# Thirteen blocks of 512 rows with seven products each, behind the 60th pair of a routed feed-forward kernel

## The chip, the cores and the metric

The kernel runs on one core of one Trainium2 chip. The metric is the device time of one execution in microseconds, lower is better. All arithmetic is in fp32.

## The reference, cut to what matters

The input `x` has 8 sequences of 3,584 tokens with 192 channels. A causal convolution of 7 taps, with softmax weights per head of 24 channels, gives each token a row. A gate then picks one of 8 experts for each token, and the row goes through that expert's two matrices.

```python
logits = np.einsum('bsd,de->bse', x, w_gate)                  # x: rows after the convolution
local_gate = 1/(1 + np.exp(-np.einsum('bsd,de->bse', x, w_local).squeeze(-1)))
# per sequence, in order of s:
e = fresh_e if s == 0 or local_gate[b, s] < 0.5 else prev_e   # fresh_e = argmax of logits
h = np.maximum(x[b, s] @ w1[e], 0.0)                          # 192 -> 1024
out[b, s] = p[e] * (h @ w2[e])                                # 1024 -> 192, p = softmax(logits)
```

There are 28,672 tokens. How many go to each expert depends on the data (3,081 to 4,253 with the inputs given).

## The kernel before

**Two kinds of work share the core.** The main work is the experts' two matrix products, on TensorE. The side work is the convolution, the routing and the sorting of rows by expert; it runs mostly on VectorE, with ScalarE, GpSimd and some small TensorE products.

**Side work.** The tokens come in 16 parts of 1,792. The first two have a start of their own. From the third on, `conv(g)` (line 387, VectorE, with a first tap on ScalarE) makes the rows of part g, and `route(g)` computes logits: four transposes `z` on VectorE (line 570), small products on TensorE (line 580), copies `ls` on ScalarE (line 585) and a transpose `lq` on VectorE (line 588). A long run of small VectorE instructions then finds each row's place. `put` scatters rows to the DRAM buffer `slots` by indirect DMAs of GpSimd (line 775), sorted by expert in units of 128 rows. `table` writes, at fixed points, which units are full by then, so that blocks can be formed before all tokens are known.

**Main work.** A block is one unit (a single) or two units (a pair) of one expert. Every block loads the whole of its expert's weights `wb` (1.5 MB) and its rows `xg`; loads are asked for three blocks ahead by SP, at indices read from the tables. The list of blocks is fixed in the program: 35 singles, 87 pairs, 20 singles, and 2 spare singles that are skipped when nothing is left for them.

For each block:

- `turn` transposes the rows on TensorE (line 359) and ScalarE copies them into `xT` (line 949), one block ahead.
- `hidden` (line 963) multiplies by the first matrix. The 192 channels are three chunks of 64; the two halves of the array, 64 rows each, compute two halves of the 1,024 hidden columns side by side. ScalarE's relu (line 968) writes `hT`.
- `output` (line 980) multiplies by the second matrix. ScalarE scales one half's sum into `o_sb` (line 988), VectorE adds the other half (line 992), and GpSimd sends each unit to its tokens' places in `out` (line 996).

PSUM has two banks for `xps`, four for `hps` and two for `yps`.

**Order.** Each engine's order is written out by hand. `step(time)` issues side work up to a budget in nominal microseconds; it is called behind `hidden`, inside `output` (1.2) and behind `output`:

```python
        step(2.4 if i == 0 else 2.1 if n == 1 else 4.2)
        output(n, wbs.pop(i), xgs.pop(i), hT)
        if i == 0:
            rest(route1)
        step(1.3 if n == 1 else 3.0)
```

`put` is issued behind a relu or a copy of the block, one to three times per pair. `ensure` asks for a block's rows, and issues more side work if a part that they need isn't placed.

Of the kernel before, what the change touches and what calls it, by code (L numbers as in the profile page):

```python
# [17 lines left out]
P = 128  # L18
# [4 lines left out]
N = B * S  # L23
# [13 lines left out]
FK = F // P  # L37
BT = 2 * UT
KT = BT // P
CAPU = N // UT  # L40
CAP = CAPU * UT
NU = (N + E * (UT - 1)) // UT
# [8 lines left out]

ONE = [_sure(min(g + 1, EARLY) * PT, UT) for g in range(NPART)]
TWO = [_sure((g + 1) * PT - ONE[-1] * UT, BT) if g >= EARLY else 0 for g in range(NPART)]


HALF = 0.5
FULL = {0: ONE[0], HALF: _sure(PT + PT // 2, UT), **{g: ONE[g] for g in range(1, NPART)}}
REST = NU - ONE[-1] - 2 * TWO[-1]  # L60
DG = 3 + D
Y0 = 2
IX = DG - 1
# [18 lines left out]
def kernel(  # L82
# [20 lines left out]
    hp = ctx.enter_context(tc.tile_pool(name="hp", bufs=1))  # L103
    op = ctx.enter_context(tc.tile_pool(name="op", bufs=2))
    xps_p = ctx.enter_context(tc.tile_pool(name="xps_p", bufs=1, space=PSUM))
    hps_p = ctx.enter_context(tc.tile_pool(name="hps_p", bufs=4, space=PSUM))
    yps_p = ctx.enter_context(tc.tile_pool(name="yps_p", bufs=2, space=PSUM))
    ctx.enter_context(tc.manual_schedule())


# [168 lines left out]
                            base=0, pattern=[[1, P]], channel_multiplier=-1)  # L279
    ii = cst.tile([P, E], I32, name="ii")  # L280
    nc.gpsimd.iota(ii, pattern=[[1, E]], base=0, channel_multiplier=0)
    pi = cst.tile([P, 2], I32, name="pi")
    nc.gpsimd.iota(pi, pattern=[[0, 2]], base=0, channel_multiplier=1)
    ti0 = cst.tile([P, NT], I32, name="ti0")
    nc.gpsimd.iota(ti0, pattern=[[1, NT]], base=0, channel_multiplier=NT)
    ef = cst.tile([P, E], F32, name="ef")
# [6 lines left out]
    nc.gpsimd.tensor_scalar(eb, ef, float(CAPU), None, Alu.mult)  # L293
    ec = cst.tile([P, E], F32, name="ec")
    nc.gpsimd.tensor_scalar(ec, ef, float(CAP), -1.0, Alu.mult, Alu.add)
    pf = cst.tile([P, 2], F32, name="pf")
    nc.gpsimd.tensor_copy(pf, pi)
    nc.gpsimd.tensor_tensor(pf[:, 1:], pf[:, 1:], pf[:, :1], op=Alu.add)
    i_of = pf[:, 0:1]
    tb0 = cst.tile([P, NB], I32, name="tb0")  # L300
    nc.gpsimd.iota(tb0, pattern=[[TB, NB]], base=0, channel_multiplier=1)
# [32 lines left out]
    pad = cst.tile([P, DG], F32, name="pad")  # L334
    nc.gpsimd.memset(pad, 0.0)
    nc.gpsimd.memset(pad.bitcast(I32)[:, IX:], N)
    nc.sync.dma_start(out=slots[DUMMY * UT:(DUMMY + 1) * UT], in_=pad)


    base = cst.tile([P, E], F32, name="base")  # L340
# [2 lines left out]
    nc.gpsimd.memset(used, 0.0)  # L343


    tab = [cst.tile([P, 3], F32, name=f"tab{k}") for k in range(3)]
    ends = [cst.tile([P, 1 + E], F32, name=f"ends{k}") for k in range(3)]
    for k in range(3):
        nc.gpsimd.memset(tab[k], 0.0)
        nc.gpsimd.memset(ends[k], 0.0)  # L350
    tabi = {}
# [402 lines left out]
    def tables(g):  # L754
        if ONE[g] > (ONE[g - 1] if g else 0):
            yield from table(0, g, 1, ONE[g])
        if TWO[g] > (TWO[g - 1] if g else 0):
            yield from table(1, g, 2, TWO[g])
        if g == NPART - 1:
            yield from table(2, g, 1, None)  # L760
            yield from fill(g)

    to_put = []
# [21 lines left out]
        tc.add_to_no_dep_group("puts", ins)  # L785
        tc.add_to_no_dep_group(f"puts{g}", ins)

    def table(kind, g, size, cap):


        end = ends[kind]
        new = sm.tile([P, E], F32, name="new")
        ni = sm.tile([P, E], I32, name="ni")
        nc.vector.scalar_tensor_tensor(new, used, -float(UT), base, Alu.mult, Alu.add)
        yield 0.2
        if cap is None:
            nc.vector.tensor_scalar(new, new, float(UT - 1), None, Alu.add)
            yield 0.2
        nc.vector.tensor_copy(ni, new)
        yield 0.2  # L800
        nc.vector.tensor_scalar(ni, ni, (UT * size).bit_length() - 1, None, Alu.arith_shift_right)
        yield 0.2
        nc.vector.tensor_copy(new, ni)
        yield 0.2
        nc.vector.tensor_copy(end[:, 0:1], end[:, E:])
        yield 0.2
        nc.vector.tensor_tensor_scan(end[:, 1:], new, new, end[:, 0:1], Alu.add, Alu.max)
        yield 0.2
        if cap is not None:
            nc.vector.tensor_scalar(end, end, float(cap), None, Alu.min)  # L810
            yield 0.2
        inn = sm.tile([P, E], F32, name="inn")
        nc.vector.tensor_scalar(inn, end[:, :E], i_of, None, Alu.is_le)
        yield 0.2
        nc.vector.scalar_tensor_tensor(inn, end[:, 1:], i_of, inn, Alu.is_gt, Alu.mult)
        yield 0.2

        row = sm.tile([P, E], F32, name="row")
        nc.vector.scalar_tensor_tensor(row, end[:, :E], -float(size), used, Alu.mult, Alu.add)
        yield 0.2  # L820
        nc.vector.tensor_tensor(row, row, eb, op=Alu.add)
        yield 0.2
        add = sm.tile([P, 3, E], F32, name="add")
        nc.vector.scalar_tensor_tensor(add[:, 0, :], row, pf[:, size - 1:size], inn,
                                       Alu.add, Alu.mult)
        yield 0.2
        nc.vector.tensor_tensor(add[:, 1, :], ef, inn, op=Alu.mult)
        yield 0.2
        nc.vector.tensor_copy(add[:, 2, :], inn)
        yield 0.2  # L830
        sums = sm.tile([P, 3], F32, name="sums")
        nc.vector.tensor_reduce(sums, add, axis=AX.X, op=Alu.add)
        yield 0.2
        nc.vector.tensor_tensor(tab[kind], tab[kind], sums, op=Alu.add)
        yield 0.2
        ti = cst.tile([P, 2], I32, name=f"tabi{kind}_{int(2 * g)}")
        if cap is None:

            no = sm.tile([P, 1], F32, name="no")
            nc.vector.tensor_scalar(no, tab[kind][:, 2:3], -float(DUMMY), float(DUMMY),  # L840
                                    Alu.mult, Alu.add)
            yield 0.2
            nc.vector.tensor_tensor(tab[kind][:, 0:1], tab[kind][:, 0:1], no, op=Alu.add)
            yield 0.2
        nc.vector.tensor_copy(ti, tab[kind][:, 0:2])
        yield 0.2
        tabi[kind, g] = ti
        nc.vector.tensor_tensor(new, end[:, 1:], end[:, :E], op=Alu.subtract)
        yield 0.2
        nc.vector.scalar_tensor_tensor(used, new, float(size), used, Alu.mult, Alu.add)  # L850
        yield 0.2

    def fill(g):
# [25 lines left out]
        nc.vector.tensor_copy(toi, to)  # L879
        yield 0.2  # L880
        for e in range(E):
            to_put.append((g, pad, toi[:, e:e + 1]))


    blocks = [(0, 1, i, next(g for g in FULL if i < FULL[g])) for i in range(ONE[-1])]
    blocks += [(1, 2, i, next(g for g in range(NPART) if i < TWO[g])) for i in range(TWO[-1])]
    blocks += [(2, 1, i, NPART - 1) for i in range(REST)]

    AHEAD = 3

# [15 lines left out]

    def load_rows(i):
        n, group = blocks[i][1], blocks[i][3]
        r = entry(i, 0, DUMMY + 1 - n)
        xg = xp.tile([P, KT, DG], F32, name="xg")  # L910
        get = nc.sync.dma_start(
            out=xg[:, :n, :].rearrange("p k d -> p (k d)"),
            in_=slots.rearrange("(r p) d -> r (p d)", p=UT)[bass.ds(r, n)]
            .rearrange("o (p x) -> (o p) x", x=n * DG))
        if group not in waited:
            waited.add(group)
            for g, ins in puts:
                if g == group:
                    tc.add_manual_dep(get.ins, ins.name, SYNC, reason="a row of the block")
        for g in FULL:  # L920
            if g > group and any(p[0] == g for p in puts):
                tc.declare_no_dep(get.ins, group=f"puts{g}", reason="not in a unit full before")
        tc.add_to_no_dep_group("gets", get.ins)
        return xg
# [48 lines left out]
    def output(n, wb, xg, hT):  # L973
# [11 lines left out]
        o_sb = op.tile([P, KT, D], F32, name="o_sb")  # L985
        y = [[yps[half][:, k * D:(k + 1) * D] for half in range(2)] for k in range(n)]
        for k in range(n):
            nc.scalar.activation(o_sb[:, k, :], y[k][0], Act.Copy, scale=xg[:, k, 0:1])  # L988

        step(1.2 if n > 1 or st["block"] else 0)  # L990
        for k in range(n):
# [9 lines left out]
            tc.add_to_no_dep_group("sent", sent.ins)  # L1001


    LEAD = 2
    LATE = 3
    st = {"block": 0, "conv": 1, "cgen": None, "route": 1, "rgen": None, "routed": 1}
# [23 lines left out]
    def route_op():  # L1030
        c = next(st["rgen"], None)
        if c is None:
            st["rgen"] = None
            st["routed"] = st["route"]
        return c

    def step(time):
# [26 lines left out]
    def rest(work):  # L1064
        for _ in work:
            pass
# [38 lines left out]
            wbs[j] = load_w(j)  # L1105
            loaded[0] += 1

    spare = blocks[len(blocks) - SPARE:]
    del blocks[len(blocks) - SPARE:]
    loaded = [0]  # L1110
    weights(AHEAD - 1)

# [25 lines left out]
    for i, (_, n, _, _) in enumerate(blocks):  # L1138
        st["block"] = i
        ensure(i)  # L1140
        weights(i + AHEAD)
        if i == LATE:
            x_in[3] = load_x(3)
        hT = hidden(n, wbs[i], xT, (1, 1) if i else (0, 0))
        if i + 1 < len(blocks):
            xT, copied = turn(blocks[i + 1][1], xgs[i + 1])
            if len(to_put) > NT // 2 and n == KT:
                put(copied)
        step(2.4 if i == 0 else 2.1 if n == 1 else 4.2)
        output(n, wbs.pop(i), xgs.pop(i), hT)  # L1150
        if i == 0:
            rest(route1)
        step(1.3 if n == 1 else 3.0)

    kind, _, at, group = spare[0]
    any_left = nc.values_load(tabi[kind, group][at:at + 1, 0:1], min_val=0, max_val=DUMMY,  # L1156
                              skip_runtime_bounds_check_because="an entry of the table")
    with tc.If(any_left < DUMMY):
        for block in spare:
            blocks.append(block)  # L1160
            i = len(blocks) - 1
            n = block[1]
            xg = load_rows(i)
            wb = load_w(i)
            xT, _ = turn(n, xg)
            output(n, wb, xg, hidden(n, wb, xT))


def _w1_layout(np, w1):
# [64 lines left out]
```

## Time and profile before

| | before |
|---|---|
| median of 3 runs | 1314.7 us (1314.69 to 1315.19) |
| profiled execution | 1326.81 us, its span 1325.1 us |
| granted TensorE clock, mean | 0.998 |
| TensorE matmul busy | 1304.4 us, 98% of the span |
| VectorE busy | 778.3 us, 59% |
| ScalarE busy | 625.2 us, 47% |
| GpSimd busy | 480.4 us, 36% |
| first pair begins, last single begins | 260.1 us, 1312.7 us |
| last side work on VectorE ends | 965.2 us |
| DMA | 325 MB, mean 245 GB/s |

A share of busy time is a mean over stages. Matmuls are pipelined and overlap, so the busy time of TensorE is no measure of how much it computes; the distance from one block's first weight load to the next's is. A group's row gives the line, the engine, the tile written and those read, the shape, the count, then the total and mean (ns) of its time, and the idle time of the engine just ahead of it with what ended it.

### The profile page before, as it was taken

The numbers are of one execution on the slowest core, as the hardware profiler recorded it, in microseconds if no ns is written. First come the engines' busy times: TensorE is split into PE (matmuls) and PEld (weight loads), VectorE is DVE, ScalarE is ACT, GpSimd is POOL, SyncE is SP. The second block draws the span as 40 slices with busy tenths as digits, with TensorE's granted clock in tenths as the row PEclk, the third lists the DMA queues.
The fourth block names the chain that finished last, engine by engine and source line by source line (L and its number), as shares of the span: only waits on it lengthen the run. The fifth ranks groups of instructions, "written<-read, shape, count | busy, mean of one in ns | idle before, by whom it ended". The sixth has DMA issues, their size and how long they took to land. (4 is left out here: it accounts for less than half of the span.)

```text
span 1325.1 us, 41356 instructions
## 1 busy us (share of the span) xinstructions
PE 1304.4 (98%) x16682; PEld 1260.9 (95%) x16682; DVE 778.3 (59%) x2434; ACT 625.2 (47%) x1571; POOL 480.4 (36%) x520
## 2 busy tenths in 40 slices
PE   9899999999999999999999999999999999999997
PEld 7799999999999999999999999999999999999997
DVE  6888898977878787878777878785610000000000
ACT  5345555544454545444545454544444444444553
POOL 4445352534343434343434343434344212211111
PEclk9999999999999999999999999999999999999999
DMA  5789999967575757575757575756565555556893
GB/s 188 283 349 391 376 365 345 394 213 266 182 275 177 290 188 277 201 260 192 271 186 273 193 271 199 267 195 210 197 211 205 189 185 188 192 187 229 313 317 131
DMA packets 67298, 325.29 MB, mean 245 GB/s; under 512 B 12576, under 2 KB 38103, under 8 KB 47650
## 3 DMA queue, kind: packets, MB, share of 16 engines
q1 hardware_dynamic: 44784, 277.41, 58.4%
q0 software_dynamic: 22320, 45.22, 9.2%
q8 instruction: 133, 2.18, 0.7%
q14 instruction: 59, 0.48, 0.1%
q10 hardware_dynamic: 2, 0.00, 0.0%
HBM read 277.29 MB, written 45.77 MB: 244 GB/s over the span
## 5 line engine op out<-in xcount | busy, mean ns | idle before, releaser
L980 PE MATMUL yps<-wb,hT 64*128 64x192 f32 x7328 | 641.0, 325 | 5.8 <-ACT hT L968 2.8
L963 PE MATMUL hps<-xT,wb 64*128 64x256 f32 (+1 forms) x6816 | 637.2, 336 | 1.7 <-issue 1.4
L963 PEld LDWEIGHTS hps<-xT,wb 64*128 64x128 f32 x6816 | 589.1, 187 | 27.2 <-issue 4.0
L980 PEld LDWEIGHTS yps<-wb,hT 64*128 64x128 f32 x7328 | 602.8, 187 | 11.1 <-issue 4.6
L996 POOL DMA_INDIRECT out_dram<-o_sb,xg x229 | 232.3, 1014 | 605.7 <-DVE o_sb L992 533.9
L968 ACT ACTIVATE hT<-hps 128x512 f32<-128x512 f32 (+1 forms) x568 | 261.9, 512 | 361.4 <-PE hps L963 246.5
L387 DVE SCALAR_TENSOR_TENSOR y_sb<-x_sb,c,y_sb 128x336 f32<-128x336 f32 x672 | 376.5, 570 | 18.9 <-issue 0.8
L992 DVE SCALAR_TENSOR_TENSOR o_sb<-yps,xg,o_sb 128x192 f32<-128x192 f32 x229 | 87.5, 414 | 467.8 <-ACT o_sb L988 461.4
L775 POOL DMA_INDIRECT slots<-y_sb,posi x228 | 231.2, 1014 | 209.3 <-ACT xT L949 114.8
L988 ACT ACTIVATE o_sb<-yps,xg 128x192 f32<-128x192 f32 x229 | 86.9, 418 | 289.8 <-PE yps L980 287.4
L949 ACT COPY xT<-xps 64x256 f32<-64x256 f32 (+4 forms) x568 | 210.8, 371 | 11.7 <-issue 1.7
L377 ACT ACTIVATE y_sb<-x_sb,c 128x336 f32<-128x336 f32 x112 | 63.7, 581 | 0.0
L359 PEld LDWEIGHTS xps<-ident,xg 64*128 64x128 f32 (+1 forms) x916 | 57.0, 124 | 5.2
L359 PE MATMUL xps<-ident,xg 64*128 64x64 f32 (+1 forms) x916 | 60.0, 217 | 0.0
L570 DVE STREAM_TRANSPOSE z<-y_sb 128x768 f32<-128x768 f32 (+1 forms) x56 | 45.4, 853 | 0.4
L596 DVE COPY lt<-lq 32x36 f32<-32x36 f32 x224 | 40.8, 182 | 3.5
L580 PE MATMUL hps<-z,wg 64*32 64x128 f32 x1344 | 24.2, 272 | 1.2 <-issue 1.2
L580 PEld LDWEIGHTS hps<-z,wg 64*32 64x32 f32 x1344 | 19.2, 105 | 4.1 <-issue 2.9
L556 PE MATMUL yps<-y_sb,hot 112*128 112x194 f32 x64 | 12.6, 353 | 1.4 <-DVE hot L550 1.1
L556 PEld LDWEIGHTS yps<-y_sb,hot 112*128 112x128 f32 x64 | 11.3, 202 | 2.1 <-DVE hot L550 1.6
L672 DVE COPY bk<-so_far 1x32 f32<-1x32 f32 x56 | 12.3, 220 | 0.7
L588 DVE STREAM_TRANSPOSE lq<-ls 128x256 f32<-128x256 f32 x14 | 6.2, 441 | 10.9 <-ACT ls L585 10.9
(236 smaller groups left out, 358.0 us busy)
## 6 DMA issues: line engine op xcount, KB each, us to landing
wb<-in_w_dram SPq DMA_DIRECT2D x138, 1536.0 KB
x_sb<-in_x_dram SPq DMA_DIRECT2D x14, 1920.0 KB
xg<-slots SPq DMA_DIRECT2D x87, 195.0 KB
wb<-in_w_dram SPq DMA_DIRECT2D x12, 512.0 KB
xg<-slots SPq DMA_DIRECT2D x53, 97.5 KB
out_dram<-o_sb,xg POOLq DMA_INDIRECT x229
slots<-y_sb,posi POOLq DMA_INDIRECT x228
x_sb<-in_xb_dram SPq DMA_DIRECT2D x4, 768.0 KB
```

The source lines that it names most:

```text
L359: nc.tensor.transpose(to, src[rows], identity=ident[rows, rows])
L377: nc.scalar.activation(cols(h), chans(h, 0), Act.Copy, scale=c[:, h, 0:1])
L387: nc.vector.scalar_tensor_tensor(cols(h), chans(h, k), c[:, h, k:k + 1], cols(h), Alu.mult, Alu.add)
L570: nc.vector.transpose(z[:, t:u, :], y_sb[:, t:u, Y0:Y0 + D])
L775: ins = nc.gpsimd.indirect_dma_start(out=slots[:, :], in_=rows, in_offset=None, out_offset=bass.IndirectOffsetOnAxis(ap=to, axis=0)).ins
L949: copied = nc.scalar.copy(a, b)
L963: nc.tensor.matmul(hps[half][:, j, w], lhsT=wb[rows, f0:f0 + P], rhs=xT[rows, d, w], start=(d == 0 and j == 0), stop=(d == KD - 1), skip_g ...
L968: relu = nc.scalar.activation(hT[:, m:m + 2, w], hps[half][:, :, w], Act.Relu)
L980: nc.tensor.matmul(yps[half][:, k * D:(k + 1) * D], lhsT=hT[rows, m, k * P:(k + 1) * P], rhs=wb[rows, WA + m * D:WA + (m + 1) * D], start= ...
L988: nc.scalar.activation(o_sb[:, k, :], y[k][0], Act.Copy, scale=xg[:, k, 0:1])
L992: nc.vector.scalar_tensor_tensor(o_sb[:, k, :], y[k][1], xg[:, k, 0:1], o_sb[:, k, :], Alu.mult, Alu.add)
L996: sent = nc.gpsimd.indirect_dma_start(out=out, in_=o_sb[:, k, :], in_offset=None, out_offset=bass.IndirectOffsetOnAxis(ap=xg.bitcast(I32)[ ...
```

## The change

The list of blocks becomes 35 singles, 60 pairs, 13 quads (4 units, 512 rows, one expert), 4 pairs, 14 singles. 20 spare singles follow behind two nested conditions, for data on which fewer quads or pairs fill up. Three tables are made at the end of routing instead of one.

In a quad the first two of the three channel chunks, two halves of its rows and two halves of the hidden columns of each array half form a product of 2 x 2 sub-matrices. It is computed by Strassen's method in Winograd's form: seven products of sums instead of eight. The third chunk stays four plain products. `combine_w` (GpSimd) forms the sums of weights, partly in place in `wb`; `combine_x` (VectorE) forms those of rows; ScalarE copies partial results out of PSUM, and VectorE adds them. From the first quad on the pools of `hps` and `yps` are closed and three tiles of two banks each, `late_p`, take their place; `xps` also takes one of the products. `xT`, the sums and the hidden pieces live in the two buffers of `x_sb` and in a buffer of `y_sb`, and rows in a ring of four places in another. The singles and pairs behind the quads use `hidden_late` and `output_late` on these buffers.

So that routing ends before the first quad, pairs issue side work with budgets of 4.8, 1.2 and 3.6 instead of 4.2, 1.2 and 3.0, and up to one more `put`.

```diff
+PAIRED = 60
+TWO = [min(PAIRED, _sure((g + 1) * PT - ONE[-1] * UT, BT)) if g >= EARLY else 0
+       for g in range(NPART)]
...
-        if g == NPART - 1:
-            yield from table(2, g, 1, None)
+        if g == LAST:
+            yield from table(2, g, 4, FOUR, 0)
+            yield from table(3, g, 2, PAIRS, 0)
+            yield from table(4, g, 1, None)
             yield from fill(g)
...
-blocks += [(2, 1, i, NPART - 1) for i in range(REST)]
+blocks += [(2, 4, i, LAST) for i in range(FOUR)]
+blocks += [(3, 2, i, LAST) for i in range(PAIRS)]
+blocks += [(4, 1, i, PADS) for i in range(REST)]
...
+    def combine_w(wb):
+        wt = room["wt"].rearrange("p (k s) -> p k s", k=3)
+        b11, b12, b21, b22 = [wb[:, k * 2 * P:(k + 1) * 2 * P] for k in range(4)]
+        nc.gpsimd.tensor_tensor(wt[:, 1, :], b22, b12, op=Alu.subtract)
+        yield
+        nc.gpsimd.tensor_tensor(b12, b12, b11, op=Alu.subtract)
+        yield
+        nc.gpsimd.tensor_tensor(wt[:, 0, :], b22, b12, op=Alu.subtract)
+        yield
+        nc.gpsimd.tensor_tensor(wt[:, 2, :], b21, wt[:, 0, :], op=Alu.subtract)
+        yield wt
...
+        nc.vector.tensor_tensor(xc[:, 0, :], xT[:, 0, one], xT[:, 0, two], op=Alu.subtract)
+        nc.vector.tensor_tensor(xT[:, 0, two], xT[:, 0, two], xT[:, 1, two], op=Alu.add)
+        nc.vector.tensor_tensor(xc[:, 1, :], xT[:, 0, two], xT[:, 0, one], op=Alu.subtract)
+        nc.vector.tensor_tensor(xc[:, 2, :], xT[:, 1, one], xc[:, 1, :], op=Alu.subtract)
+        nc.vector.tensor_tensor(xc[:, 3, :], xT[:, 2, one], xT[:, 2, two], op=Alu.subtract)
...
+        def times(to, a, b, first=False):
+            for j in range(2):
+                for half, rows in halves():
+                    ins = nc.tensor.matmul(to[:, half, j, :], lhsT=b[rows, j * P:(j + 1) * P],
+                                           rhs=a[rows, :], start=(first and j == 0), stop=True,
+                                           skip_group_check=True)
+            return ins
+
+        times(xb, a11, b11, True)
+        nc.scalar.copy(h11, xb)
+        times(yb, s1, t1, True)
+        times(yb, a23, b32)
+        nc.scalar.copy(h22, yb)
+        times(xb, s2, t2)
+        nc.scalar.copy(h12, xb)
+        put(times(wbk, a12, b21, True))
+        times(wbk, a13, b31)
+        nc.vector.tensor_tensor(h11, wbk, h11, op=Alu.add)
+        nc.scalar.activation(h11, h11, Act.Relu)
+        put(times(xb, s3, t3))
+        nc.vector.tensor_tensor(h22, xb, h22, op=Alu.add)
+        nc.scalar.activation(h22, h22, Act.Relu)
+        times(yb, s4, b22)
+        put(times(yb, s5, b32))
+        at = turn_next()
+        times(xb, a22, t4)
+        wt = weights_next()
+        next(wt)
+        put(times(xb, a23, b31))
+        next(wt)
+        nc.vector.tensor_tensor(h12, yb, h12, op=Alu.add)
+        nc.scalar.activation(h12, h12, Act.Relu)
+        nc.scalar.activation(h21, xb, Act.Relu)
+        return [[h11, h12], [h21, h22]], at, wt
...
-            step(2.4 if i == 0 else 2.1 if n == 1 else 4.2)
+            step(2.4 if i == 0 else 2.1 if n == 1 else 4.8)
...
-        step(1.3 if n == 1 else 3.0)
+            step(1.3 if n == 1 else 3.6)
+            continue
+        if i == FIRST:
+            banks.close()
+            for k in range(3):
+                late_p.append(ctx.enter_context(tc.tile_pool(name=f"late{k}", bufs=1, space=PSUM)))
```

`output_late` computes the output of a quad in two parts of two units each, with one tile of two banks per part; between the parts it calls `combine_x` for the next quad and issues the last step of `combine_w`.

## The prediction

> **What bounds the kernel now.** I read the busy shares and slices of the page first, then the table of waits, then the order of instructions inside one block, and last the groups of a stretch in which side work runs.
>
> ```profile
> PE 1304.4 (98%) x16682; PEld 1260.9 (95%) x16682; DVE 778.3 (59%) x2434; ACT 625.2 (47%) x1571; POOL 480.4 (36%) x520
> ...
> PE   9899999999999999999999999999999999999997
> ...
> DVE  6888898977878787878777878785610000000000
> ```
>
> TensorE is full in every slice; VectorE carries routing and convolution until slice 29 and then idles. Between 260 and 965 us the table of waits has for TensorE's matmuls only 0.9 us. A share alone would not settle it, since busy matmuls overlap, so here is the order of weight loads in one late pair (start, length, engine, line) and in one late single:
>
> ```profile
> 1048.88 5.10 PEld L963 LDWEIGHTS hps<-xT,wb 64*128 64x128 f32 x48
> 1054.01 0.45 PEld L359 LDWEIGHTS xps<-ident,xg 64*128 64x128 f32 x8
> 1054.40 5.18 PEld L980 LDWEIGHTS yps<-wb,hT 64*128 64x128 f32 x64
> 1059.55 0.57 PEld L963 LDWEIGHTS hps<-xT,wb 64*128 64x128 f32 x6
> ```
>
> ```profile
> 1296.39 2.81 PEld L963 LDWEIGHTS hps<-xT,wb 64*128 64x128 f32 x48
> 1299.12 0.23 PEld L359 LDWEIGHTS xps<-ident,xg 64*128 64x128 f32 x4
> 1299.29 2.58 PEld L980 LDWEIGHTS yps<-wb,hT 64*128 64x128 f32 x32
> 1301.84 0.35 PEld L963 LDWEIGHTS hps<-xT,wb 64*128 64x128 f32 x3
> ```
>
> A pair takes 1059.55 - 1048.88 = 10.67 us without a hole: 5.13 hidden, 0.39 turning, 5.15 output. The hidden part is 48 matmuls; the two 64-row halves run side by side, so 24 slots of 5.13/24 = 0.214 us for 256 columns. A single takes 5.445 us, against 5.333 for half a pair. So in the part that is changed time is what TensorE must stream, and nothing else.
>
> [...] In the trace the three accumulating steps of a hidden half all run at one pace. [...]
>
> **The change, part by part.**
>
> *Removed and added TensorE work.* Behind pair 60 there are 74 units of 128 rows: before 27 pairs and 20 singles, after 13 quads, 4 pairs and 14 singles (routing the reference's inputs fills all 13 quads and 4 pairs, so the spare blocks stay skipped). Two pairs need 12 hidden products of 256 rows by 256 hidden columns by 64 channels; `seven` issues 11. A product is 2 x 2 matmuls, two passes each, so 4 slots: 4 x 0.214 = 0.855 us. A quad is 11 x 0.855 = 9.40, turning 2 x 0.39 = 0.78, output 2 x 5.15 = 10.30: 20.48 us against 21.33. 13 x 0.855 = **11.1 us** gained, all on TensorE's path. Six singles fewer: 6 x (5.445 - 5.333) = **0.7 us**. The 14 logit insertions (1.8 us each) stay.
>
> *Can the evictions keep pace inside a quad?* The accumulator `xb` is read after the 1st and 4th product and overwritten by later ones. What ScalarE does in the pair above:
>
> ```profile
> 1049.24 0.73 ACT L988 ACTIVATE o_sb<-yps,xg 128x192 f32<-128x192 f32 x2 [2.59 <-PE yps L980]
> 1051.89 1.08 ACT L968 ACTIVATE hT<-hps 128x512 f32<-128x512 f32 x2 [1.92 <-PE hps L963]
> 1054.42 1.08 ACT L968 ACTIVATE hT<-hps 128x512 f32<-128x512 f32 x2 [1.45 <-PE hps L963]
> 1055.39 1.75 ACT L949 COPY xT<-xps 128x256 f32<-128x256 f32 x4
> ```
>
> It starts 0.36 to 0.45 us after TensorE is through; 512 elements take 0.54 us, 256 in the late singles 0.33, so 1,024 some 0.96 (estimate). From a quad's start: product 1 ends at 0.86, copy 1.26 to 2.22; product 4 is due at 2.57. Product 3 ends at 2.57, copy 2.97 to 3.93; product 4 ends at 3.42, copy 3.93 to 4.89; product 7 is due at 5.13. Margins: 0.3 and some 0.15 us with 0.1 us from ScalarE back to TensorE. [...] ScalarE's sum: 7 x 0.96 + 2.6 turning + 1.5 output = 10.8 of 20.5 us.
>
> *GpSimd's `combine_w`.* No such row exists. [...] the nearest row, the one-input copy of 512 (line 223), takes 0.655. Four per quad beside four indirect DMAs of 1.0 us: 7 of 20.5 us, each a block ahead of its reader except the fourth, written behind the first two sends and read 9 us later. Even at 2 us each it stays covered. I take nothing; bounds 0 and 0.3 us a quad.
>
> So a quad loses 0 to 0.3 us at product 7; I take 0.08, **1.1 us** in all (bounds 0 and 4).
>
> *Moved: the side work.* Per pair 4.8 + 1.2 + 3.6 = 9.6 units are issued instead of 8.4, so the last routing stands six pairs ahead of the first quad (before: 23 pairs ahead of the singles), a part per five pairs instead of six. VectorE over six pairs and one part, 469 to 534.66 us:
>
> ```profile
> L387 DVE SCALAR_TENSOR_TENSOR y_sb<-x_sb,c,y_sb 128x336 f32<-128x336 f32 x48 | 26.9, 569 | 1.3
> ...
> L992 DVE SCALAR_TENSOR_TENSOR o_sb<-yps,xg,o_sb 128x192 f32<-128x192 f32 x12 | 4.5, 413 | 11.5 <-ACT o_sb L988 11.5
> ```
>
> It is occupied 65.66 - 11.5 = 54.2 us. With ten evictions instead of twelve (0.37 each) 53.4 us remain, 55 if the gaps under 0.12 us between instructions count in full; TensorE needs 5 x 10.67 + 1.83 = 55.2. VectorE goes from 83% to 97-99% and still does not bind; the eviction may lag 3.7 us (output of the next block starts 5.5 us later, the eviction ends 1.6 us after its block) before TensorE waits. The 14 scatters per five pairs cost GpSimd 24 x 1.3 = 31 of 55 us. I take 0 (bounds -1 and +15).
>
> *Boundary, DMA, start.* Reused row buffers and PSUM banks were freed several pairs earlier; the first quad's rows (390 KB) are asked for some 15 us before they are turned. SP's weight loads queue behind row loads that now wait for the sends of the block before last: about 3 us of delay in a lead of three blocks (16 us among singles), so no cost. Weights moved fall from 47 x 1.5 to 31 x 1.5 MB. At the start GpSimd gets four memsets (0.1 us each) and a little arithmetic, beside waits of 4.7 us there; the pad rows grow by 290 KB. Together 0 (bounds -0.5 and +1.5).
>
> **Sum.** 11.1 + 0.7 - 1.1 = 10.7 us. The profiled execution took 1326.8 us (span 1325.1, 1.7 around it), the median without profile 1314.7, 0.9% less; scaled, 10.6. **Predicted 1304 us**; the profiled span should be near 1314.5.
>
> **Rivals.**
> 1. *VectorE becomes the bound of the pair stage, slower.* Place: evictions at line 992 of pairs 1 to 49. For it: 97-99% in the sum, and the logits' transpose now stands directly behind an eviction, where it waits about 1.2 us for TensorE and ScalarE. Against: lag may reach 3.7 us, and convolution rows cost 0.57 us whether GpSimd is busy or not. It decides once a part needs over 55.2 us; all gain is gone at 56.4 (ten parts x 1.2). At 5% more than 55 (57.8) ten parts lose 26, less the lag, some 22: 1326 us.
> 2. *The quads stall at the evictions.* If a copy takes 1.3 us instead of 0.96, product 7 waits 0.6 us, 13 x 0.6 = 8: about 1311. For it: the smallest margin; against: the slope from 256 to 512 elements.
> 3. *Whole-tile dependences.* `xT`, `xc` and `wt` share one row buffer. If a reader of one waited for writers of the others, `combine_w` (last part behind the sends) would hold up each quad by a few us: 1320 or more. The built program's waits name the right engines only at products 2, 4 and 10, which speaks against it.
>
> **Numbers.** Forecast 0.70; a gain over it (pair-stage hiccups of some 2 us go away) 0.02; rival 2, partly or in full, 0.15 (0.03 of it within 0.2%); rival 1 0.10 (0.03 still faster, 0.02 within, 0.05 slower); rival 3 0.03, slower. 0.2% (2.6 us) is about what a measurement of this kernel can tell from no change. Slower by more: 0.08; within: 0.05; faster: 0.87. The range reaches from all margins holding with some gain to rival 2 in full: 1300.5 to 1311.
>
> **What would show it.** Weight loads of the changed kernel's line 1152 (88 per quad) in 9.4 us without waits; quads 20.5 us apart; the first gap at product 7, released by ScalarE's copy of `h12`, if any. Pairs still 10.67 us, and idle before VectorE's eviction (now line 1030) nearly gone in that stage. It is wrong if pairs are longer than 10.7 us (rival 1), if product 10 waits for VectorE, or if quads exceed 21.3 us.

## The result, and the profile after

| | before | after |
|---|---|---|
| median without profile | 1314.7 us (1313.93 to 1315.19, 4 runs) | 1304.16 us (1303.46 to 1305.35, 4 runs) |
| ratio, 95% interval | | 0.9921 (0.9904 to 0.9938) |
| profiled execution, its span | 1326.8, 1325.1 us | 1305.35, 1303.6 us |

The time fell by 10.5 us; 10.7 were forecast. That agreement has to be read with care. Run again on chips 10, 7 and 1, the same two kernels gave ratios of 1.0004, 0.9964 and 1.0007 (below; the chip of this first comparison is not on record), so the gain of the quads is certain and what the denser side work costs is not. The two profiled executions lie 21.5 us apart, the medians 10.5, and the span, forecast near 1314.5 us, is 1303.6. That forecast scaled from the profile before, which took 12 us more than the median before, while the profile after took 1 us more than the median after; so the two profiles can hardly have been taken in like conditions. Of the 21.5 us, 7.6 stand ahead of the first pair (252.5 us after, 260.1 before), where other traces of one and the same kernel differ as much. So I compare by stages.

The busy row and two rows of slices of the page after:

```profile
PE 1284.2 (99%) x16434; PEld 1220.6 (94%) x16434; DVE 846.3 (65%) x2526; ACT 651.1 (50%) x1482; POOL 523.1 (40%) x577
...
PE   9899999999999999999999999999999999999997
...
DVE  5989898988988899998999996801333333330000
```

TensorE stays full; its matmuls overlap (in the quads 376 ns each, eight of them in 0.85 us). VectorE's side work ends in slice 26 instead of 29, at a higher level; the row of 3 behind it is the work in the quads.

One quad in the timeline after (start, length, engine, line; PEld is a weight load, 187 ns each):

```profile
1012.17 2.51 PEld L1152 LDWEIGHTS ps<-x_sb,wb 64*128 64x128 f32 x24
1013.46 1.01 ACT L1158 COPY x_sb<-ps 128x1024 f32<-128x1024 f32 x1 [0.18 <-PE ps L1152]
1014.71 0.84 PEld L1152 LDWEIGHTS ps<-x_sb 64*128 64x128 f32 x8
1015.19 1.01 ACT L1161 COPY y_sb<-ps 128x1024 f32<-128x1024 f32 x1 [0.71 <-PE ps L1152]
1015.57 1.70 PEld L1152 LDWEIGHTS xps<-x_sb,wb 64*128 64x128 f32 x16
1016.10 1.02 ACT L1163 COPY x_sb<-ps 128x1024 f32<-128x1024 f32 x1
1017.30 0.84 PEld L1152 LDWEIGHTS ps<-x_sb 64*128 64x128 f32 x8
...
1018.64 0.73 POOL L1115 TENSOR_TENSOR x_sb<-wb 128x256 f32<-128x256 f32 x1 [2.36 <-PE ps L1152]
...
1018.93 1.21 DVE L1169 TENSOR_TENSOR y_sb<-ps,y_sb 128x1024 f32<-128x1024 f32 x1
...
1019.89 0.68 PEld L383 LDWEIGHTS xps<-ident,y_sb 64*128 64x128 f32 x16
...
1022.13 7.88 PEld L1196 LDWEIGHTS ps<-wb,x_sb 64*128 64x128 f32 x96
```

A bracket gives the idle time ahead of a row and what ended it. No PEld row has one: TensorE never waits in the quad. The copy at line 1163 ends at 1017.12 and product 7, which adds onto the accumulator that this copy reads, begins at 1017.30: the predicted narrow place, with a margin of 0.18 us. VectorE's second add (line 1169), which reads the same accumulator behind product 7, ends at 1020.14, and product 10, which adds onto it again, begins at 1020.51: 0.37 us. Adding onto what stands in a bank costs nothing extra here: products 1 to 3, of which the third adds onto the second, take 2.54 us (0.85 each), product 4, which adds onto the first, 0.86. From 1012.17 to 1022.13 are 9.96 us for hidden part and turning, the output takes 10.46; the next quad's first load comes 20.42 us after this one's, and so it is between all 13.

VectorE's groups over five pairs and one part, 428.46 to 483.5 us after (count, then busy us and mean ns, then the idle time ahead of them):

```profile
L411 DVE SCALAR_TENSOR_TENSOR y_sb<-x_sb,c,y_sb 128x336 f32<-128x336 f32 x48 | 26.8, 570 | 2.4 <-ACT y_sb L401 1.1
L1030 DVE SCALAR_TENSOR_TENSOR o_sb<-yps,xg,o_sb 128x192 f32<-128x192 f32 x11 | 4.1, 407 | 0.2 <-ACT o_sb L1024 0.2
```

The eviction's 11.5 us of waiting are down to 0.2: in this stretch VectorE is always behind, as forecast. It waits for 1.3 us in all, so that it is occupied for 53.7 us, and the part still takes 55.04 us, which is TensorE's time. In the first 50 pairs VectorE's eviction starts 0.46 us behind ScalarE's in the trace before, and 0.97 us in the trace after (medians; at most 2.2).

### The profile page after: what moved, and what is told of

It reads as the page before. It is cut to its first block, busy times and chain, and to the rows that moved or that the text cites. A ratio compares the mean times of both kernels' runs of the same rounds, so it can differ in the third digit from the quotient of the medians.

```text
span 1303.6 us, 40830 instructions
## 1 busy us (share of the span) xinstructions
PE 1284.2 (99%) x16434; PEld 1220.6 (94%) x16434; DVE 846.3 (65%) x2526; ACT 651.1 (50%) x1482; POOL 523.1 (40%) x577
## 3 DMA queue, kind: packets, MB, share of 16 engines
q8 instruction: 131, 2.15, 0.7%
## 4 chain that ended last, share of the span: by engine, by line
PE 96%; DVE 3%; issue 0%; POOL 0%; POOLq 0%; ACT 0%; DVEq 0%
PE yps L1016 31%; PE hps L999 31%; PE ps L1196 15%; PE ps L1152 8%; PE ps L1103 4%; PE xps L383 2%; PE xps L1152 2%; PE hps L604 2%; DVE y_sb L411 1%; PE hps L233 1%; PE hps L178 0%; DVE hot L574 0%; PE hps L256 0%; PE yps L264 0%; DVE run L475 0%
## 5 line engine op out<-in xcount | busy, mean ns | idle before, releaser
L1016 PE MATMUL yps<-wb,hT 64*128 64x192 f32 x4960 | 429.8, 325 | 3.2 <-DVE o_sb L1030 2.4
L999 PE MATMUL hps<-xT,wb 64*128 64x256 f32 (+1 forms) x4560 | 425.9, 338 | 1.9 <-DVE at L503 1.2
L999 PEld LDWEIGHTS hps<-xT,wb 64*128 64x128 f32 x4560 | 378.7, 188 | 33.9 <-issue 3.9
L1016 PEld LDWEIGHTS yps<-wb,hT 64*128 64x128 f32 x4960 | 405.7, 187 | 4.6 <-DVE o_sb L1030 2.7
L411 DVE SCALAR_TENSOR_TENSOR y_sb<-x_sb,c,y_sb 128x336 f32<-128x336 f32 x672 | 375.6, 569 | 28.4 <-ACT y_sb L401 10.5
L1004 ACT ACTIVATE hT<-hps 128x512 f32<-128x512 f32 (+1 forms) x380 | 176.4, 516 | 244.5 <-PE hps L999 244.5
L1214 POOL DMA_INDIRECT out_dram<-o_sb,y_sb x74 | 76.4, 1032 | 237.5 <-DVE o_sb L1209 218.7
L1196 PE MATMUL ps<-wb,x_sb 64*128 64x192 f32 x1952 | 165.0, 323 | 0.0
L1196 PEld LDWEIGHTS ps<-wb,x_sb 64*128 64x128 f32 x1952 | 159.3, 187 | 0.6
L985 ACT COPY xT<-xps 128x256 f32<-128x256 f32 (+3 forms) x380 | 142.0, 374 | 10.6 <-PE xps L383 4.8
L1152 PEld LDWEIGHTS ps<-x_sb,wb 64*128 64x128 f32 x624 | 59.0, 187 | 7.3
L1103 PEld LDWEIGHTS ps<-x_sb,wb 64*128 64x128 f32 x864 | 59.4, 188 | 0.9 <-issue 0.2
```

What stands on the lines that cost most here:

```text
L411: nc.vector.scalar_tensor_tensor(cols(h), chans(h, k), c[:, h, k:k + 1], cols(h), Alu.mult, Alu.add)
L985: copied = nc.scalar.copy(a, b)
L999: nc.tensor.matmul(hps[half][:, j, w], lhsT=wb[rows, f0:f0 + P], rhs=xT[rows, d, w], start=(d == 0 and j == 0), stop=(d == KD - 1), skip_g ...
L1004: relu = nc.scalar.activation(hT[:, m:m + 2, w], hps[half][:, :, w], Act.Relu)
L1016: nc.tensor.matmul(yps[half][:, k * D:(k + 1) * D], lhsT=hT[rows, m, k * P:(k + 1) * P], rhs=wb[rows, WA + m * D:WA + (m + 1) * D], start= ...
L1103: nc.tensor.matmul(hps[:, half, j, :], lhsT=wb[rows, f0:f0 + P], rhs=xT[rows, d, :], start=(d == 0 and j == 0), stop=(d == KD - 1), skip_g ...
```

## The stages of all traces

Read from the first weight loads of the blocks. "Extra" is what the pairs ahead of the first quad (or, before, ahead of the 61st pair) take over 10.67 us each and 1.78 us for each logits insertion; "rest" runs from there to the last matmul, "tail" from the last matmul to the end of the span. A dash stands where no chip is on record.

| trace | chip | early singles | pairs | extra | rest | tail |
|---|---|---|---|---|---|---|
| before | - | 213.9 | 659.1 | 2.9 | 399.1 | 6.8 |
| after | - | 207.9 | 657.6 | -0.4 | 384.4 | 9.1 |
| b1_before | 7 | 217.3 | 659.3 | 3.1 | 399.8 | 6.8 |
| a2_after | 7 | 218.2 | 665.5 | 7.5 | 385.6 | 9.1 |
| a1_after | 10 | 218.7 | 669.5 | 11.5 | 385.3 | 8.9 |
| a3_after | 1 | 220.3 | 669.8 | 11.8 | 385.1 | 8.9 |
| e2_pace | 10 | 220.7 | 665.9 | 7.9 | 397.6 | 6.7 |
| e1_twelve | 10 | 217.1 | 669.5 | 11.5 | 396.3 | 9.1 |
| e4_copy2 | 7 | 213.7 | 665.2 | 7.2 | 395.7 | 10.3 |
| e6_p70 (70 pairs) | 7 | 215.7 | 770.1 | 5.4 | 284.0 | 10.0 |
| e5_p56 (56 pairs) | 10 | 221.6 | 670.9 | 55.6 | 426.7 | 8.6 |
| e7_spread | 1 | 220.4 | 686.4 | 28.4 | 385.0 | 10.6 |
| e8_bundle | 1 | 219.9 | 674.7 | 18.4 | 401.4 | 6.7 |
| e9_two | 15 | 219.1 | 681.2 | 23.2 | 385.0 | 8.7 |

Against the two traces of the kernel before, "rest" falls by 13.5 to 15.4 us in the four traces of the changed kernel. 1.8 of it is a logits insertion that now stands among the 60 pairs.

## Experiments: the gain

**a1_after: the changed kernel again.** No edit.

> The changed kernel once more, beside the others on one chip. Theory (TensorE's stream alone sets the time behind pair 60): 1304.2 us, 10.5 us below the kernel before; the sum of block distances in the trace says 12.6. Rival (part of the gap between the two profiles, 7.5 us in the stage of early singles, belongs to the change): the ratio would move towards 0.985.

1333.1 us, before 1332.0 on that chip: 1.0004 (0.9992 to 1.0017). Quads again 20.42 us apart, but the pairs take 12 us more than in the first trace. The top rows of the table of waits of TensorE's weight loads between first pair and first quad (total us, times, longest); first the trace after, then a1_after:

```profile
PEld hps L999 <- issue: 1.4, 7, 0.2
PEld hps L604 <- issue: 1.3, 6, 0.2
PEld yps L1016 <- issue: 0.3, 1, 0.3
```

```profile
PEld yps L1016 <- issue: 9.5, 24, 1.1
PEld hps L999 <- issue: 1.4, 7, 0.2
```

24 holes (stops between two weight loads), 9.5 us, lie inside the output products, where TensorE waits for nothing that the profile shows ("issue"). VectorE's eviction does not appear.

**e1_twelve: quads without the seven products.** The sums are left out and the hidden part is twelve plain products:

```diff
-        times(yb, s1, t1, True)
-        times(yb, a23, b32)
+        times(xb, a12, b21)
+        times(xb, a13, b31)
...                              (12 products, no combine_w, no combine_x)
```

> Quads stay, with their buffers, banks and pace, but their hidden part is 12 plain products instead of 11; the sums of weights and of rows are gone. Theory: one product more per quad, 4 slots of 0.214 us = 0.855 us, 13 x 0.855 = 11.1 us: 1315.3 us, and quads 21.3 us apart. Rival (the gain comes from larger blocks: 31 weight loads instead of 47, half the switches between hidden, turning and output, six singles fewer): 1304 to 1306 us.

1340.91 us, 1.0064 (1.0048 to 1.0079). Quads 21.28 us apart: 13 blocks take 276.4 us instead of 265.4, so one product per quad is worth 0.85 us, as forecast (0.855). The medians differ by 7.8 us, where a1_after's own runs lie up to 8.6 us apart. The pairs' extra is 11.5 us, the same as in a1_after: it has nothing to do with the quads' arithmetic.

**e4_copy2: the narrow place.** The copy of `h12` is made twice.

```diff
         nc.scalar.copy(h12, xb)
+        nc.scalar.copy(h12, xb)
```

> The changed kernel with the copy of h12 made twice (the same data to the same place). The margin ahead of product 7 is 0.18 us in the trace of the changed kernel, the copy 1.02 us. Theory (the evictions pace the quad at product 7 and the margin is what the trace shows): the copy of h12 ends some 0.95 us later, product 7 waits for ScalarE by 0.8 to 1.0 us in each quad, quads are 21.2 to 21.4 us apart, the time grows by 10 to 13 us against the changed kernel. Rival (what counts is ScalarE's share of the quad, 11.2 of 20.4 us, and later products catch up): quads stay within 0.2 us of 20.42.

1333.4 us, 9.6 more than the changed kernel on that chip; quads 21.23 us apart. In its timeline:

```profile
1013.94 1.02 ACT L1163 COPY x_sb<-ps 128x1024 f32<-128x1024 f32 x1
1014.99 1.01 ACT L1164 COPY x_sb<-ps 128x1024 f32<-128x1024 f32 x1
...
1016.06 0.73 PEld L1152 LDWEIGHTS ps<-x_sb 64*128 64x128 f32 x8 [0.94 <-ACT x_sb L1164]
```

From the end of that copy to TensorE's next load are 0.06 us, where the prediction allowed 0.1. One more copy of 1.05 us costs 0.81 us a quad, so 0.2 us of slack were there. A small share of busy time (ScalarE 11.2 of 20.4 us) is no protection where one product waits for one copy. Rival 2, the stall at the evictions, was a matter of 0.2 us.

## Experiments: what the pace costs

**e2_pace: the pace alone.** The kernel before with the new budgets.

```diff
-        step(2.4 if i == 0 else 2.1 if n == 1 else 4.2)
+        step(2.4 if i == 0 else 2.1 if n == 1 else 4.8)
...
-        step(1.3 if n == 1 else 3.0)
+        step(1.3 if n == 1 else 3.6)
```

> The kernel before with the new budgets alone (4.8, 1.2, 3.6 per pair), nothing else. Theory (VectorE is nearly full but lags less than its buffers allow): no change, 1314.7 us within 1.5, pairs still 10.67 us, wait of VectorE before its eviction nearly gone. Rival (the denser side work makes VectorE bind the pairs): 3 us or more slower. Second rival (the gain of the change came from the pace): 3 us or more faster.

1337.94 us, 1.0041 (1.0024 to 1.0058): 6 us slower on a chip where I had expected none. The pace costs, without any quad; extra 7.9 us.

**e5_p56: denser still, quads earlier.** 15 quads behind 56 pairs, budgets 5.2 and 4.0, four scatters behind the hidden halves in the last 11 pairs.

```diff
-PAIRED = 60
+PAIRED = 56
-            hT = hidden(n, wbs[i], xT, (1, 1) if i else (0, 0))
+            hT = hidden(n, wbs[i], xT, (2, 2) if i > FIRST - 12 else (1, 1) if i else (0, 0))
...                              (budgets)
```

> The changed kernel with PAIRED = 56: 15 quads instead of 13, 4 pairs fewer; budgets 5.2, 1.2, 4.0 and up to two more scatters per pair in the last 11 pairs so that all rows are placed in time. Theory: two quads more at 0.915 us each against pairs (21.33 - 20.42): 1.8 us faster, 1302.3. Rival (rows of the first quads come late, since scatters and sends share GpSimd's queue): a gap of several us before the first quad, 1304 to 1310.

1371.12 us, 1.028 (1.0255 to 1.0305). 56 pairs take as long as 60. It looks like VectorE as the bound, and is not: TensorE's waits in the pairs name VectorE nowhere,

```profile
PEld yps L1016 <- issue: 40.8, 73, 1.3
PEld hps L999 <- issue: 1.7, 6, 0.6
```

and in the pairs the trace's granted clock fell to half three times, for 17 us together (mean of the whole trace 0.992; 0.995 in a1_after). 44 us of holes in weight loads (logits with them) and some 8.5 for the clock (an estimate, half of the 17) make most of the 55.6. Some 25 us of it fall into the last 11 pairs with their extra scatters, some 31 into the 45 pairs ahead, where only the budgets are denser.

**Where the holes stand.** In a3_after, the timeline of one (only its rows of GpSimd and TensorE's weight loads, two of ScalarE and one of VectorE):

```profile
400.61 0.73 ACT L1024 ACTIVATE o_sb<-yps,xg 128x192 f32<-128x192 f32 x2 [2.19 <-PE yps L1016]
...
402.96 0.74 DVE L1030 SCALAR_TENSOR_TENSOR o_sb<-yps,xg,o_sb 128x192 f32<-128x192 f32 x2
...
403.65 0.99 POOL L1034 DMA_INDIRECT out_dram<-o_sb,xg  x1 [5.72 <-DVE o_sb L1030]
...
404.94 0.99 POOL L1034 DMA_INDIRECT out_dram<-o_sb,xg  x1 [0.30 <-DVE offs L758]
...
405.77 2.74 PEld L1016 LDWEIGHTS yps<-wb,hT 64*128 64x128 f32 x33
...
406.24 0.96 POOL L801 DMA_INDIRECT slots<-y_sb,posi  x1 [0.30 <-issue]
...
407.51 0.96 POOL L801 DMA_INDIRECT slots<-y_sb,posi  x1 [0.30 <-issue]
...
408.04 1.74 ACT L985 COPY xT<-xps 128x256 f32<-128x256 f32 x4 [1.17 <-remote]
...
409.39 1.79 PEld L1016 LDWEIGHTS yps<-wb,hT 64*128 64x128 f32 x22 [0.89 <-issue]
```

GpSimd issues four indirect DMAs one straight behind the other, two sends and two scatters; behind the fourth TensorE stops for 0.89 us. GpSimd had waited 5.72 us for VectorE's eviction, which began 2.35 us behind ScalarE's (400.61 to 402.96) where the kernel before has 0.46 throughout; so the sends ran into the scatters. I counted such runs (starts under 1.75 us apart) between the first pair and 930 us, and how many have a hole behind them: over 0.4 us between the starts of two of TensorE's weight loads, logits apart, within 4 us of the run's last start. The last four rows are of runs described further down:

| trace | runs of three, with hole | runs of four and more, with hole |
|---|---|---|
| before, b1_before | 56, 0 each | 2, 2 each |
| a1_, a2_, a3_after | 32, 0 each | 21, 14; 21, 10; 21, 15 |
| e1_twelve, e4_copy2 | 32, 0 each | 21, 16; 21, 10 |
| e2_pace, e5_p56 | 39, 0; 19, 0 | 11, 6; 33, 24 |
| after, first trace | 32, 0 | 21, 0 |
| e6_p70 | 46, 0 | 11, 2 |
| e8_bundle | 0, 0 | 56, 11 |
| e7_spread | 48, 6 | 2, 2 |
| e9_two | 33, 3 | 3, 3 |

Denser side work makes runs of four (2 before, 21 after), and on chips 1, 7 and 10 they go with holes. The same pairs are long there: block 82, counted from 0, takes 12.35, 12.10 and 12.28 us in a1_, a2_ and a3_after. In the first trace of the changed kernel such runs leave none, though 15 of the 21 are six long. So three experiments (e7, e8, e9) move the scatters alone.

**a3_after: the changed kernel beside the next two.** No edit.

> The changed kernel beside the next two, on their chip. In the earlier traces TensorE's idle time without a visible cause stands nearly always behind four or more indirect DMAs that GpSimd issues one straight behind the other (12 of 19 such runs of four in a1_after, 9 of 19 in a2_after, 0 of some 30 runs of three in each). Theory (runs of four cost): about 20 runs of four between the first pair and the first quad, some 10 of them with a hole of over 0.4 us in TensorE's weight loads, 60 pairs in 665 to 670 us, ratio 0.996 to 1.000. Where no holes stand behind the runs, 60 pairs take 658 us and the ratio is about 0.992.

1332.11 us, 1.0007 (0.9994 to 1.002); holes as expected.

**e7_spread: no scatter straight behind the sends.**

```diff
-        if n == KT and len(to_put) > NT - 2:
+        if n == KT and len(to_put) > 3:
-            hT = hidden(n, wbs[i], xT, (1, 1) if i else (0, 0))
+            hT = hidden(n, wbs[i], xT, ((0, 1) if n == KT else (1, 1)) if i else (0, 0))
-                if len(to_put) > NT // 2 and n == KT:
+                if len(to_put) > 3 and n == KT:
```

> The changed kernel, quads and pace untouched; of a pair's two to four scatters none is issued behind the first hidden half, where the two sends of the block before have just been issued; they go behind the second half, behind the turning copy and behind the output. Theory (runs of four indirect DMAs cost): hardly any run of four is left, the holes go with them, 60 pairs in about 659 us (60 x 10.67 + 10 x 1.83), 5 to 9 us under a3_after, ratio to before about 0.991. Rival (VectorE near its limit is what costs, through late evictions): the pairs take as long as in a3_after, within 2 us.

1349.9 us, 1.0127 (1.0109 to 1.0145): a miss, with one part right. Runs of four fell to 2, and the pairs away from the logits take 10.67 us again (median of all 10.67; 10.84 in a3_after). VectorE's evictions lag further than in a3_after (median 1.48 us behind ScalarE's, at most 4.9, against 0.80 and 2.4), so a late eviction alone doesn't lengthen a pair. But the blocks with the logits, which the changed order of issue sets a block earlier, take up to 16.7 us instead of 12.5. The timeline there:

```profile
434.55 1.07 PEld L604 LDWEIGHTS hps<-z,wg 64*32 64x32 f32 x77 [0.22 <-PE yps L1016]
...
435.49 0.95 POOL L801 DMA_INDIRECT slots<-y_sb,posi  x1 [2.31 <-ACT o_sb L1024]
...
436.07 0.16 PEld L604 LDWEIGHTS hps<-z,wg 64*32 64x32 f32 x3 [0.45 <-issue]
...
436.86 0.10 PEld L604 LDWEIGHTS hps<-z,wg 64*32 64x32 f32 x1 [0.62 <-issue]
437.59 0.17 PEld L604 LDWEIGHTS hps<-z,wg 64*32 64x32 f32 x5 [0.62 <-issue]
...
438.34 0.18 PEld L604 LDWEIGHTS hps<-z,wg 64*32 64x32 f32 x6 [0.58 <-issue]
```

77 of the 96 small loads pass in 1.07 us; then TensorE goes on in handfuls, one every 0.75 us, for 4 us. The first stop begins behind a single scatter beside short instructions, and two sends follow; so "runs of four" is not the whole rule, and neither is it in the table above, where six runs of three have a hole.

**e8_bundle: the kernel before, its scatters put behind the sends.**

```diff
-        hT = hidden(n, wbs[i], xT, (1, 1) if i else (0, 0))
+        hT = hidden(n, wbs[i], xT, ((2, 0) if n == KT else (1, 1)) if i else (0, 0))
```

> The kernel before with its own pace; in each pair both scatters are issued behind the first hidden half, straight behind the two sends, instead of one behind each half. No work is added. Theory (runs of four indirect DMAs cost): some 50 runs of four instead of 2, at the 0.2 to 0.4 us a run seen in a1_after and a2_after 10 to 20 us slower, ratio 1.007 to 1.015. Rival (VectorE's occupancy is what costs): VectorE still has 17 per cent to spare, the time stays within 2 us.

1350.37 us, 1.013 (1.0112 to 1.0148): 18 us slower with not one instruction added and VectorE as free as before. The size is as expected, its place is not: 56 runs of four have only 11 holes outside the logits, and each logits block grew from some 12.5 to 13.8 us. TensorE's waits in the pairs:

```profile
PEld hps L580 <- issue: 9.2, 18, 0.6
PEld yps L980 <- issue: 6.6, 26, 0.9
```

**b1_before and a2_after: both kernels again, on a third chip.** No edit.

> The kernel before once more, with a profile, beside the changed kernel. If the dense pace of the side work is what took the gain away in a1_after, TensorE's idle time without a visible cause ('issue') between the first pair and the 61st is smaller here than the 16 us of a1_after (about 8 us or less), and the 60 pairs take about 662 us against 669.5 there. If instead the whole chip is slower, the 60 pairs take about 669 us here as well and idle 'issue' time is alike.

1330.97 us, one run; pairs of 659.3 us and 5 us of holes in the loads, so the first case of the two expected.

> The changed kernel once more, to see how far the first two comparisons (0.9921 and 1.0004) scatter. Theory (the quads give 12 us, and the dense pace before them costs TensorE idle time that depends on the chip): quads 20.42 us apart again, and a ratio between 0.990 and 1.001, low where the pairs keep 10.67 us and high where they don't. Rival (the pace costs nothing, and a1_after was an accident): 0.991 to 0.993 here.

1323.79 us, 0.9964 (0.9951 to 0.9977): between the other two comparisons, as its extra of 7.5 us is. Here both kernels were traced on one chip: the extra grows by 4.4 us.

**e6_p70: the old pace, quads later.** Eight quads behind pair 70, budgets of before.

```diff
-PAIRED = 60
+PAIRED = 70
-            step(2.4 if i == 0 else 2.1 if n == 1 else 4.8)
+            step(2.4 if i == 0 else 2.1 if n == 1 else 4.2)
-            step(1.3 if n == 1 else 3.6)
+            step(1.3 if n == 1 else 3.0)
```

> The changed kernel with the pace of before (budgets 4.2 and 3.0) and the quads behind the 70th pair: 8 quads, 4 pairs and 14 singles behind it. The side work ends seven pairs ahead of the first quad in both. Theory (the pace costs, the quads pay): 8 x 0.91 + 0.7 for the singles = 8.0 us under before on any chip, a ratio of about 0.994; faster than the changed kernel where that shows no gain, some 4 us slower than it where that gains 10.5. Rival (something in the layout of the changed kernel costs, whatever the pace): on a chip where the changed kernel gives 1.000, this one gives 1.003 or more.

1326.34 us, 0.9987 (0.9978 to 0.9996), on the chip where the changed kernel gave 0.9964. Against b1_before's trace it gains 6.8 us in what follows pair 70, loses 1.8 in the pairs and 3.2 in the tail. The 8.0 expected left out the tail.

**e9_two: two scatters a pair, logits in their old place.**

```diff
-        if n == KT and len(to_put) > NT - 2:
+        if n == KT and len(to_put) > NT - 4:
-            hT = hidden(n, wbs[i], xT, (1, 1) if i else (0, 0))
+            hT = hidden(n, wbs[i], xT, ((0, 1) if n == KT else (1, 1)) if i else (0, 0))
-                if len(to_put) > NT // 2 and n == KT:
+                if len(to_put) > 0 and n == KT:
```

> The changed kernel, quads and pace untouched; of the scatters of a pair one goes behind the second hidden half and one behind the turning copy, and a third behind the output only while more than 10 are waiting, so that the pair ahead of a logits block issues only two; the logits keep the places they have in the changed kernel (in e7_spread they stood a block earlier, and TensorE's holes fell into them). Theory (what costs is GpSimd's indirect DMAs issued straight behind the two sends): next to no run of four ahead of pair 55, ordinary pairs at 10.67 us and logits blocks at 12.5, 60 pairs in 658 to 661 us, ratio to before 0.989 to 0.993. Rival 1 (VectorE near its limit costs): 60 pairs in 665 to 670 us as in the changed kernel, ratio 0.996 to 1.001. Rival 2 (the holes only move, as in e7_spread): ordinary pairs at 10.67 us, but logits blocks at 14 us or more, ratio 1.000 to 1.013.

1342.05 us, 1.0083 (1.0058 to 1.0108): rival 2. Ordinary pairs take 10.67 us (median), but the logits blocks 65, 70 and 75 take 14.5, 16.9 and 14.5 us and hold up the blocks right behind them, and block 93, beside a run of eight with six scatters in it, takes 17.2.

**What is shown, and what is open.** Shown: when and beside what GpSimd issues its indirect DMAs sets how long TensorE stands still, by 18 us in e8_bundle with the same work; and VectorE need not be full for it. Where it is, as in the a3_after lines, its late eviction makes the sends meet the scatters; that this is how the denser pace costs is likely, but no run tried it alone. Not shown: why TensorE stops, and whether it is the issue or the transfer of the rows that counts, since both moved together. The page of a1_after has a DMA queue of kind `instruction`, 2.15 MB in 131 packets:

```profile
q8 instruction: 131, 2.15, 0.6%
```

The first trace of the changed kernel has the same 131 packets and 2.15 MB, and no hole behind its runs; a packet takes 0.98 us (median) there and 0.96 in a1_after. Of the 18 holes outside the logits in a1_after, six begin within 3 us behind the start of a packet, where chance alone would give five. So nothing there ties the holes to that queue; its records don't tell which engine a packet is for. Open also why the first trace has no holes behind 21 such runs. No version of mine beats the changed kernel.

## Why the prediction was right, and where only by balance

1. **The products (11.1 us): right, a little low.** 13 x (21.33 - 20.42) = 11.9 us measured. Hidden part and turning of a quad took 9.96 us instead of 9.40 + 0.78 (turning 16 tiles takes 0.62), the output 10.46 instead of 10.30. e1_twelve confirms 0.85 us for a product.
2. **Singles (0.7): right**; in the first trace another 0.5 us comes from the first late single (5.97 us before, 5.45 after). In a1_, a2_ and a3_after it takes 5.97 to 6.00 us again, so this is not the change's doing.
3. **Loss at product 7 (1.1): too much.** The margin was 0.18 us where 0.15 was estimated, and it held: loss 0. ScalarE's copy took 1.01 us (estimate 0.96). What the sums on VectorE and GpSimd take, the trace before did not show; after, a VectorE add of 1,024 elements takes 1.21 to 1.23 us, the five steps of `combine_x` 0.41 to 0.43 each in the quad above (2.1 together, under the second half of the output), and the four steps of `combine_w` 0.73 to 0.75 (medians), against 0.655 for the nearest row before. None of them holds TensorE up.
4. **"Boundary, DMA, start ... Together 0": the step that failed.** The tail was left out. The last row of the timeline and the span, after and then before:

```profile
core 0 of [0], span 1303.6 us
...
1295.66 0.97 POOL L1214 DMA_INDIRECT out_dram<-o_sb,y_sb  x1 [4.31 <-DVE o_sb L1209]
```

```profile
core 0 of [0], span 1325.1 us
...
1319.51 0.97 POOL L996 DMA_INDIRECT out_dram<-o_sb,xg  x1 [4.30 <-DVE o_sb L992]
```

The span ends 7.0 us behind the last send instead of 4.6, so 2.4 us are lost; the traces with the changed layout have a tail of 8.6 to 10.6 us, those with the old one 6.7 to 6.8. GpSimd's last steps show where (POOLq is its instruction sequencer; shortest/median/longest in ns, then first and last start in us), after and then before:

```profile
L1438 POOLq INC_SWDGE_SEM  x1: 924/924/924, 1298.5 to 1298.5; - x1
L1506 POOLq DRAIN  x3: 40/107/3101, 1299.4 to 1303.1; - x3
```

```profile
L1158 POOLq INC_SWDGE_SEM  x1: 929/929/929, 1320.1 to 1320.1; - x1
L1230 POOLq DRAIN  x3: 40/107/3101, 1321.1 to 1324.7; - x3
```

The longest drain, of 3.1 us, is the first of the three and starts when the step ahead of it is through. After, that step waits for the semaphore of the last send and starts at 1298.46, when the send's data has landed (1298.43). Before, it waits for an earlier send's semaphore and starts at 1320.12, so that the last send lands (1321.76) while the drain is under way. It is so in all fourteen traces: with the changed layout the step starts 1.5 to 3.3 us behind the last send's end and the span ends 6.4 to 8.4 us behind it; with the old one the step starts 0.4 us ahead of the send's end and the span ends 4.5 to 4.6 us behind it. So the tail is one landing that the drain no longer covers. That the two nested conditions bring this order of waits about is likely, but was not tried alone.

By stages of the two traces, what follows pair 60 falls by 14.7 us, of which 1.8 is the logits insertion that moved, and the tail grows by 2.4: 10.5 us, the whole difference of the medians. In the forecast's terms the sum becomes 11.9 + 0.7 + 0.5 - 2.4 = 10.7 us. It is the forecast's figure by luck: what was put too low (0.8 at the products, 0.5 at the singles, 1.1 at product 7) happens to equal the tail.

5. **The side work ("I take 0 (bounds -1 and +15)"): right in the first comparison** (extra -0.4 after, and the sum above leaves nothing for it; the 2.9 before are of the profile that took 12 us more than the timed runs), wrong on other chips: by 4.4 us on chip 7, and by 8 to 9 on chips 10 and 1 if the kernel before has the 3.1 of chip 7 there. The upper bound covered it, the reason given did not: I priced VectorE's lag, and "24 x 1.3 = 31 of 55 us" of GpSimd as a share. The runs point to the order and the neighbours of those 24, not to their sum.
6. **The rivals.** Rival 1: VectorE did get as full as worked out (occupied 53.7 us of 55.0, forecast 53.4 to 55), and does not bind; a convolution row takes 0.57 us beside a busy GpSimd and beside an idle one (medians, traces before and after). Rival 2 stayed 0.2 us away. Rival 3: in no trace of the changed kernel does a quad take more than 20.42 us, so nothing of that kind holds one up.

## What to carry to other kernels

A gain in what TensorE must stream could be read off ahead here (11.1 us forecast for the products, 11.9 measured), if each eviction is placed on the clock of the block and the narrowest one is named. When you make room for it, look at how close together other engines' DMAs are then issued: a mean share of 57% on GpSimd says nothing on runs of four. And compare stage by stage, down to the tail, on more than one chip: here the total was right while several terms were not.

## Of the hardware, not expected

- TensorE stops, for up to 1.3 us at a time (e5_p56; 1.1 in a1_after and a3_after), behind many runs of four or more indirect DMAs that GpSimd issues back to back (10 to 15 of 21 in a1_, a2_ and a3_after, on chips 10, 7 and 1; 11 of 56 in e8_bundle), and behind none of three in the eleven traces in which the scatters keep their places. Where they were moved (e7_spread, e9_two) it stops behind some runs of three too. Among short instructions (the 96 logits products of e7_spread) it goes on in handfuls every 0.75 us. The first trace shows none of this.
- GpSimd's last drain takes 3.1 us, whether or not the last send is still under way; a wait for that send ahead of it goes with 1.8 to 3.8 us more at the end of the program (spans ending 6.4 to 8.4 us behind the last send against 4.5 to 4.6).
- The kernel before takes 1314.7 us in the first comparison, whose chip is not on record, and 1328 to 1332 us on chips 1, 7, 10 and 15.
